# Reading wq in eight transfers of sixteen rows instead of one of 128

## The chip, the cores and the metric

The kernel runs on one core of a Trainium2 chip. The metric is the device time of one execution in microseconds. The profile is that of one execution, taken by the hardware profiler. Engines in it: PE is TensorE (PEld its weight loads), DVE VectorE, ACT ScalarE, POOL GpSimd, SP SyncE, which here only issues transfers. A "q" behind an engine's name is its sequencer. The core has sixteen DMA engines, which all queues share. SP's transfers are on one queue (q1 in the profile), ACT's on another (q10).

## The reference

A gated mix of two blocks for a single decode token, batch 2, all in bf16. Block A is attention over a cache of 16,384 positions with 32 heads of 128; block B is an MLP with a layer norm. The caches dominate the bytes: K and V have 268 MB each.

```python
def _A_ref(x, k_cache, v_cache, wq, wo):
    B, Sq, D = x.shape                       # 2, 1, 1024
    H, Dh = 32, 128
    q = transpose((x @ wq).reshape(B, Sq, H, Dh), 0, 2, 1, 3)
    scores = jnp.einsum("bhqd,bhkd->bhqk", q, k_cache) * (Dh ** -0.5)
    p = softmax(scores, axis=-1)
    o = jnp.einsum("bhqk,bhkd->bhqd", p, v_cache)
    return transpose(o, 0, 2, 1, 3).reshape(B, Sq, H * Dh) @ wo

g = sigmoid((x * gate_w).sum(-1, keepdims=True))
a = _A_ref(x, A_k_cache, A_v_cache, A_wq, A_wo)
b = _B_ref(x, B_w1, B_w2, B_w3, B_w4)        # layer norm, gelu, shifts, two more products
return g * a + (1 - g) * b
```

wq is 1024 x 4096 bf16, 8.39 MB; wo is as large. w2 has 2.10 MB, w3 and w4 7.34 MB each, w1 2.10 MB.

## The kernel before, in words

**Memory.** One tile, `mem`, holds 128 partitions of five cells of 32 KB. A unit of K or V (two heads of one batch) is 8.39 MB, that is 64 KB a partition, two cells. K of batch 0 uses cells 0 and 1, K of batch 1 cells 1 and 2, V cells 3 and 4. So K of the other batch can be loaded as soon as DVE has turned the half of K that lies in cell 1. wq lies first in cells 3 and 4 (64 KB a partition: partition p holds rows 8p to 8p+7 of wq), then w3, then V. w2 is in cell 2.

**Transfers.** SP issues wq (line 91, in `load_weight`), then K of head pair 0 and batch 0, called K(0,0) here (line 109), and waits with w3 (line 91) until PE has read wq out of the same cells. Then come K(0,1), V(0,0) and so on, each as soon as its cells are free. ACT's queue takes x and the gate's weights (lines 97 and 98) and w2. Transfers of one queue are worked off in the order in which they were issued.

**The start.** PE turns x, then waits for wq and multiplies (`rows4`, line 203, 64 matmuls for q). ACT and DVE bring q into the form that the scores need. Then a chain of small steps computes the gate, the layer norm, the product with w2, the second layer norm and xn2T; it ends on DVE with the copy `lane_b`, ahead of the first transpose of K. Each engine takes its instructions in program order (`in_order`).

**The loop.** For each of 16 head pairs and both batches: DVE transposes K by chunks (line 427), PE multiplies with q (line 433), a softmax on DVE, ACT and PE, then PE multiplies with V (line 487). The first unit runs ahead of the loop. The last pair also loads wo, w4 and w1 into freed cells, and PE computes the output from these (line 394).

**Waiting.** Tile's own tracking gives each transfer a semaphore. A tail load of the kernel uses another way, in `load_tail`: the transfer raises a semaphore of the kernel's own, is taken out of the tracking by a group, PE waits on the semaphore by hand, and `declare_fence` says which instruction of PE closes the group. The change uses the same for wq.

Of the kernel before, what the change touches and what calls it, by code (L numbers as in the profile page):

```python
# [23 lines left out]
def kernel(  # L24
# [15 lines left out]
    nc = tc.nc  # L40
    P = nc.NUM_PARTITIONS
    B, Sq, D = A_x.shape
    _, H, Sk, Dh = A_k_cache.shape
# [3 lines left out]
    KC = D // P  # L47
# [32 lines left out]
    def region(cell, elements, offset=0):  # L80
        at = cell * CELL + offset
        return mem[:, at : at + elements]

    def load_weight(W, cell, offset=0, pieces=None, queue=nc.sync):
        K, N = W.shape
        dst = region(cell, K // P * N, offset)
        src = W.rearrange("(p r) n -> p (r n)", p=P)
        r = 0
        for n in pieces or (K // P,):
            at = slice(r * N, (r + n) * N)  # L90
            queue.dma_start(out=dst[:, at], in_=src[:, at])
            r += n
        return dst.rearrange("p (r n) -> p r n", n=N)

    wq = load_weight(A_wq, 3)
    rows = const.tile([B + 1, D], BF16, name="rows")
    nc.scalar.dma_start(out=rows[0:B], in_=A_x.rearrange("b s n -> (b s) n"))
    nc.scalar.dma_start(out=rows[B : B + 1], in_=gate_w.unsqueeze(0))
# [14 lines left out]
    def load_v(hp, b, cell=V_CELL):  # L113
# [7 lines left out]
        out=ident_s[:], in0=ident_f[:], scalar1=-scale, scalar2=None, op0=ALU.mult  # L121
# [10 lines left out]
        out=mask4[:], in_=mask4[:], compare_op=ALU.is_ge, fill=0.0,  # L132
# [3 lines left out]
        out=mask4[:], in_=mask4[:], compare_op=ALU.is_ge, fill=0.0,  # L136
# [11 lines left out]
        out=lmat[:].rearrange("p (g h k) -> p g h k", h=2, k=4),  # L148
        in_=hm2[:].unsqueeze(1).unsqueeze(3).to_broadcast([P, P // 8, 2, 4]),
# [5 lines left out]
        out=lane[:],  # L155
        in_=ident_f[:].rearrange("p (c k) -> p k c", k=QP),
# [5 lines left out]
    for g in range(Q4):  # L162
        nc.vector.tensor_scalar(
            out=spread[:, g],
# [4 lines left out]
    oacc = [ops.tile([P, 4 * Dh], FP32, name=f"oacc{k}") for k in range(2)]  # L169
# [19 lines left out]

    def rows4(acc, actT, weight, R, at, n, G, added=None):
        for g in range(Q4 if added is not None else 0):
            nc.tensor.matmul(
                acc[QP * g : QP * g + B, 0:n],
                lhsT=ident_b[0:B, 0:B],
                rhs=added[:, g * G + at : g * G + at + n],
                start=True,
                stop=False,
            )  # L200
        for r in range(R):
            for g in range(Q4):
                nc.tensor.matmul(  # L203
                    acc[QP * g : QP * g + B, 0:n],
                    lhsT=actT[:, r, :],
                    rhs=weight[:, r, g * G + at : g * G + at + n],
                    start=(r == 0 and added is None),
                    stop=(r == R - 1),
                )

    def turned(wide, C):
        t = mlp.tile([P, C, QP], FP32, tag="turn", name="turn")
        nc.vector.transpose(  # L213
            out=t[:].rearrange("p c k -> p (c k)"), in_=wide.rearrange("p c k -> p (c k)")
        )
        return t[:, :, 0:B]

    def layer(actT, weight, k, added=None):
        rows4(oacc[k], actT, weight, KC, 0, G1, G1, added)
        wide = mlp.tile([P, KC, QP], FP32, tag="wide", name="wide")  # L220
        nc.scalar.activation(
            out=wide[:], in_=oacc[k][:, 0:G1].rearrange("p (i r) -> p r i", r=KC), func=ACTF.Copy
        )
        return turned(wide[:], KC)
# [11 lines left out]
    nc.vector.tensor_copy(out=rowsT[:], in_=rows_ps[:])  # L236
    xT = rowsT[:, :, 0:B]

    for k in range(2):
        rows4(oacc[k], xT, wq, KC, k * 4 * 512, 512, 512)  # L240
    NV = 4
    qb = const.tile([P, 2, 2, 2, B, NV], BF16, name="qb")
    for k in range(2):
        wide = mlp.tile([P, 16, QP], FP32, tag="wide", name="wide")
        nc.scalar.activation(  # L245
            out=wide[:].rearrange("p (c e) i -> p c e i", e=2),
            in_=oacc[k][:].rearrange("p (c i e) -> p c e i", i=QP, e=2),
# [15 lines left out]
    for e in range(2):  # L263
        half = slice(e * HALF, (e + 1) * HALF)
        nc.vector.tensor_copy(
            out=qdu[half].rearrange("p u v -> p (u v)"),
            in_=qdps[half, e].rearrange("p k g n -> p (k g n)"),
# [83 lines left out]
    for shift in (1, -1, 2, -2):  # L351
# [10 lines left out]
        out=x1_rows[:], in_=oacc[1][:, 0:G1], func=ACTF.Copy, scale=omg_row[:, 0:1]  # L362
# [3 lines left out]
    def mlp_third(w3):  # L366
        for k in range(2):
            rows4(oacc[k], xn2T, w3, KC, k * (G3 // 2), G3 // 2, G3)
        wide3 = mlp.tile([P, FC, QP], FP32, tag="wide", name="wide")
        for k in range(2):  # L370
            nc.scalar.activation(
                out=wide3[:, :, k * (QP // 2) : (k + 1) * (QP // 2)],
                in_=oacc[k][:, 0 : G3 // 2].rearrange("p (i r) -> p r i", r=FC),
                func=ACTF.Copy,
            )
        h2 = gelu_T(turned(wide3[:], FC), FC)
        nc.vector.tensor_tensor(out=h2T[:], in0=h2[:], in1=spread_batch(omg, FC), op=ALU.mult)
# [340 lines left out]
```

## Time and profile before

| what | us |
|---|---|
| median of three runs | 1329.3 (1329.28 to 1329.56) |
| profiled execution | 1329.34 |
| its span, first to last instruction | 1327.5 |
| wq, from issue to landing | 26.0 |
| w3, from issue to landing | 32.1 |
| K, from issue to landing, median of 32 | 27.8 |
| SP waiting on DVE's transposes before it issues K, 31 times | 509.1 |

The core read 572.53 MB from HBM in this execution, 431 GB/s over the span. A DMA share of 1.00 means that the sixteen DMA engines worked all the time in a stretch. Packets count in the window in which they start, so a window of one or two microseconds can show a share above 1 or a rate above the mean. An idle time is put down to what came last before the waiting instruction; idle time of an engine that is not the bottleneck costs nothing.

### The profile page before, as it was taken

The numbers are of one execution on the slowest core, as the hardware profiler recorded it, in microseconds if no ns is written. First come the engines' busy times: TensorE is split into PE (matmuls) and PEld (weight loads), VectorE is DVE, ScalarE is ACT, GpSimd is POOL, SyncE is SP. The second block draws the span as 40 slices with busy tenths as digits, with TensorE's granted clock in tenths as the row PEclk, the third lists the DMA queues.
The fourth block names the chain that finished last, engine by engine and source line by source line (L and its number), as shares of the span: only waits on it lengthen the run. The fifth ranks groups of instructions, "written<-read, shape, count | busy, mean of one in ns | idle before, by whom it ended". The sixth has DMA issues, their size and how long they took to land. (4 is left out here: it accounts for less than half of the span.)

```text
span 1327.5 us, 12951 instructions
## 1 busy us (share of the span) xinstructions
PE 753.8 (57%) x4948; PEld 329.0 (25%) x4948; DVE 648.1 (49%) x507; ACT 131.9 (10%) x205; POOL 11.9 (1%) x48
## 2 busy tenths in 40 slices
PE   2555566655556665555666555566655556665553
PEld 0222222222222222222222222222222222222222
DVE  1654445554444555444455544445554444555420
ACT  0011111011111100111110011111001111100110
POOL 0000000000000000000000000000000000000000
PEclk9677788777778877777887777788777778877777
DMA  9999999999999999999999999999999999999998
GB/s 411 441 435 421 433 440 425 436 436 440 423 434 438 430 434 432 440 423 436 436 438 427 432 440 425 434 438 438 425 434 438 429 432 436 440 423 436 436 430 373
DMA packets 10676, 572.68 MB, mean 431 GB/s; under 512 B 1189, under 2 KB 1189, under 8 KB 1578
## 3 DMA queue, kind: packets, MB, share of 16 engines
q1 hardware_dynamic: 10512, 570.43, 99.4%
q10 hardware_dynamic: 154, 2.11, 0.4%
q8 instruction: 8, 0.13, 0.0%
q14 instruction: 2, 0.02, 0.0%
HBM read 572.53 MB, written 0.00 MB: 431 GB/s over the span
## 5 line engine op out<-in xcount | busy, mean ns | idle before, releaser
L433 PE MATMUL S<-KT,qw 128*128 128x512 bf16 x2048 | 545.5, 416 | 357.1 <-DVE KT L427 357.0
L427 DVE STREAM_TRANSPOSE KT<-mem 128x2048 f32<-128x2048 f32 x256 | 570.6, 2282 | 261.7 <-DMA mem<-in_A_k_cache_dram 205.6
L433 PEld LDWEIGHTS <-qw 128*128 128x128 bf16 x2048 | 215.9, 105 | 678.6 <-issue 473.6
L487 PE MATMUL oacc<-mem,pt 128*8 128x512 bf16 x2048 | 117.9, 383 | 6.6 <-DMA mem<-in_A_v_cache_dram 6.6
L458 ACT ACTIVATE Dm<-ident_s,m 128x128 f32<-128x128 f32 x32 | 12.9, 402 | 970.1 <-PE oacc L487 943.5
L471 ACT ACTIVATE pt<-St,nb 64x256 bf16<-64x256 f32 x64 | 89.7, 1401 | 60.3 <-DVE nb L469 59.4
L509 DVE TENSOR_SCALAR o_all<-misc,g_rep 128x2 f32 (+1 forms) x32 | 7.0, 219 | 162.1 <-PE misc L505 162.1
L480 PE MATMUL misc<-rs,lmat 128*128 128x1 f32 x64 | 18.8, 363 | 107.9 <-ACT pt L471 61.3
L487 PEld LDWEIGHTS <-pt 128*8 128x8 bf16 x2048 | 47.3, 87 | 74.4 <-issue 22.4
L505 PE MATMUL misc<-lane,osb 128*128 128x2 f32 x256 | 33.5, 253 | 45.3 <-ACT osb L500 45.3
L481 DVE RECIPROCAL rinv<-misc 128x1 f32<-128x1 f32 x32 | 5.4, 168 | 108.6 <-PE misc L480 60.5
L454 DVE STREAM_TRANSPOSE St<-S 128x512 f32<-128x512 f32 x32 | 22.9, 717 | 66.4 <-PE L487 64.5
L505 PEld LDWEIGHTS misc<-lane,osb 128*128 128x128 f32 x256 | 31.2, 192 | 61.1 <-ACT osb L500 31.7
L480 PEld LDWEIGHTS misc<-rs,lmat 128*128 128x128 f32 x64 | 16.1, 312 | 114.3 <-ACT pt L471 64.8
L500 ACT ACTIVATE osb<-oacc,rinv 128x512 f32<-128x512 f32 x32 | 22.0, 687 | 87.2 <-PE oacc L487 87.2
L471 ACT ACTIVATION_READ_ACCUMULATOR pt<-St,nb 64x1 f32 x64 | 30.6, 478 | 0.0
L381 POOL TENSOR_TENSOR qw<-qdu,mask 128x16 bf16<-128x16 bf16 x32 | 7.3, 261 | 1135.8 <-PEq L677 1074.7
L469 DVE TENSOR_REDUCE nb<-misc 64x1 f32<-64x64 f32 x64 | 14.2, 222 | 6.1 <-PE misc L464 3.6
L213 DVE STREAM_TRANSPOSE turn<-wide 128x512 f32<-128x512 f32 (+2 forms) x4 | 3.0, 745 | 26.3 <-ACT wide L245 21.3
L464 PE MATMUL misc<-Dm,ones_f 128*128 128x128 f32 x64 | 15.7, 329 | 0.0
L203 PE MATMUL oacc<-mem,rowsT 128*2 128x512 bf16 x64 | 6.2, 570 | 15.7 <-DMA mem<-in_A_wq_dram 15.7
L456 DVE TENSOR_REDUCE m<-St 128x1 f32<-128x256 f32 x32 | 13.4, 420 | 1.1
(98 smaller groups left out, 85.1 us busy)
## 6 DMA issues: line engine op xcount, KB each, us to landing
mem<-in_B_w_dram SPq DMA_DIRECT2D x1, 7168.0 KB, 32.1
mem<-in_B_w_dram SPq DMA_DIRECT2D x1, 4096.0 KB, 41.2
mem<-in_B_w_dram SPq DMA_DIRECT2D x1, 2304.0 KB, 32.2
mem<-in_B_w_dram ACTq DMA_DIRECT2D x1, 2048.0 KB, 33.1
mem<-in_B_w_dram SPq DMA_DIRECT2D x1, 1280.0 KB, 35.0
mem<-in_B_w_dram SPq DMA_DIRECT2D x1, 768.0 KB, 33.5
mem<-in_A_k_cache_dram SPq DMA_DIRECT2D x32, 27.8
mem<-in_A_v_cache_dram SPq DMA_DIRECT2D x32, 32.4
```

The lines of the kernel that those rows point to most:

```text
L427: nc.vector.transpose(out=kt[:], in_=Kc.rearrange("p j d -> p (j d)").bitcast(FP32))
L433: nc.tensor.matmul(S, lhsT=qw[b][:, v, NG - 1 - m : NG - 1 - m + P], rhs=ktb[:, half * GT : (half + 1) * GT, w, :, e], start=(first and n ...
L454: nc.vector.transpose(out=st[:].rearrange("p j r -> p (j r)"), in_=S[:])
L456: nc.vector.tensor_reduce(out=m[:], in_=st[:, :, 0:NG], axis=AX.XY, op=ALU.max)
L458: nc.scalar.activation(out=Dm[:], in_=ident_s[:], func=ACTF.Copy, scale=m[:, 0:1])
L464: nc.tensor.matmul(R_ps[:], lhsT=ones_f[:], rhs=Dm[:], start=True, stop=True)
L469: nc.vector.tensor_reduce(out=nb[rows], in_=R_ps[rows, rows], axis=AX.X, op=ALU.min)
L471: nc.scalar.activation(out=pts[b][rows, :, e, :].rearrange("p (m a) k -> p a k m", a=GT // 4), in_=st[rows, :, 0:NG].rearrange("p (a k) m ...
L480: nc.tensor.matmul(tot_ps[:], lhsT=lmat[:], rhs=rs[:], start=True, stop=True)
L487: nc.tensor.matmul(oacc[b][QP * q : QP * q + 8, :], lhsT=pts[b][:, g].rearrange("p h k -> p (h k)"), rhs=V[:, 4 * g : 4 * g + 4, :].rearra ...
L500: nc.scalar.activation(out=osb[:], in_=oacc[b][:], func=ACTF.Copy, scale=rinvs[b][:, 0:1])
L505: nc.tensor.matmul(ot[:], lhsT=osb[:, k * Dh : (k + 1) * Dh], rhs=lane[:, k : k + 5 : 4], start=(k == 0), stop=(k == 3),)
```

## The change

wq is no longer read by `load_weight` in one transfer of 128 rows (one row of 65,536 bytes a partition), but by a loop of eight transfers on the same queue, SP's. Transfer k takes the sixteen partitions k, k+8, ..., k+120, and the same rows of the source. All eight count on one semaphore, `wq`, 16 each; PE waits for 128 before the first matmul with wq. The transfers and the matmuls are in the group `wq`, so Tile adds no waits between them, and the last matmul closes the group for the loads that come into these cells later. The bytes, their place and the matmuls are the same.

```diff
-    wq = load_weight(A_wq, 3)
+    wq_all = region(3, KC * H * Dh)
+    wq_src = A_wq.rearrange("(p r) n -> p (r n)", p=P)
+    wq_sem = tc.alloc_semaphore("wq")
+    ROWS_OF = P // 16
+    for k in range(ROWS_OF):
+        dma = nc.sync.dma_start(out=wq_all[k:P:ROWS_OF], in_=wq_src[k:P:ROWS_OF])
+        dma.then_inc(wq_sem, 16)
+        tc.no_tile_sem_insts.add(dma.ins.name)
+        tc.add_to_no_dep_group("wq", dma.ins)
+    wq = wq_all.rearrange("p (r n) -> p r n", n=H * Dh)
...
-    def rows4(acc, actT, weight, R, at, n, G, added=None):
+    def rows4(acc, actT, weight, R, at, n, G, added=None, group=None):
...
-                nc.tensor.matmul(
+                mm = nc.tensor.matmul(
...
+                if group is not None:
+                    tc.declare_no_dep(mm.ins, group=group, reason="own semaphore")
+        return mm
...
+    nc.tensor.wait_ge(wq_sem, 16 * ROWS_OF)
     for k in range(2):
-        rows4(oacc[k], xT, wq, KC, k * 4 * 512, 512, 512)
+        mm = rows4(oacc[k], xT, wq, KC, k * 4 * 512, 512, 512, group="wq")
+    tc.declare_fence(mm.ins, group="wq")
```

## The prediction

> **What bounds the kernel now.** I read the page's busy shares and its DMA lines first, then stretches of the span for the rate stage by stage, then the first 60 us in order of time, then SP's own waits. The page, its span and DMA lines:
>
> ```profile
> span 1327.5 us, 12951 instructions
> PE 753.8 (57%) x4948; PEld 329.0 (25%) x4948; DVE 648.1 (49%) x507; ACT 131.9 (10%) x205; POOL 11.9 (1%) x48
> ...
> DMA  9999999999999999999999999999999999999998
> ...
> q1 hardware_dynamic: 10512, 570.43, 99.4%
> q10 hardware_dynamic: 154, 2.11, 0.4%
> ```
>
> No compute engine passes 57%, while the sixteen DMA engines are taken for 99.8% of their span by SP's queue (q1) and ACT's (q10). The chain that ended last gives DMA only 32%, because it often steps through compute to an issue that did not hold the engines up; the shares of the DMA engines decide here. Stretches of the span (columns: stretch, us, busy time of each engine, PE clock, DMA share, GB/s):
>
> ```profile
> 1.80:26.80 25.00, 0.63 (x8) 0.65 (x9) 4.15 (x12) 1.28 (x1) 2.11 (x5) 1.00 1.02 431
> 26.80:48.00 21.20, 11.48 (x114) 5.84 (x114) 6.12 (x31) 2.22 (x5) 1.63 (x3) 0.71 0.99 426
> 48.00:65.00 17.00, 13.35 (x47) 5.15 (x47) 15.02 (x7) 0.00 (x0) 0.00 (x0) 0.77 1.01 439
> 65.00:300.00 235.00, 139.51 (x871) 59.66 (x872) 124.17 (x93) 24.02 (x38) 1.37 (x6) 0.80 1.00 433
> 300.00:800.00 500.00, 289.50 (x1799) 126.03 (x1792) 255.26 (x182) 50.66 (x78) 3.17 (x14) 0.78 1.00 434
> ```
>
> The rate is one flat ceiling, 433 to 434 GB/s at a DMA share of 1.00, whether wq, a cache or a weight is read. So a row of 65,536 B takes one engine 65,536 / (433/16 GB/s) = 2.42 us. wq has 128 such rows, 8 an engine: 19.4 us. w2 (2.10 MB) takes 4.8 us, K(0,0) 19.4 us and w3 (7.34 MB) 17.0 us. Nothing later can make up for time lost here: from 65 to 1284 us the engines have no idle share to take it back from.
>
> The first 60 us in order of time (start, duration, engine, line, operation; in brackets the idle time before and what ended it):
>
> ```profile
> 0.80 0.38 SPq L91 DMA_DIRECT2D mem<-in_A_wq_dram  x1
> ...
> 1.25 0.42 SPq L109 DMA_DIRECT2D mem<-in_A_k_cache_dram  x1
> ...
> 26.89 6.17 PE L203 MATMUL oacc<-mem,rowsT 128*2 128x512 bf16 x64 [15.69 <-DMA mem<-in_A_wq_dram]
> ...
> 32.89 0.33 SPq L91 DMA_DIRECT2D mem<-in_B_w_dram  x1
> ...
> 48.04 4.51 DVE L427 STREAM_TRANSPOSE KT<-mem 128x2048 f32<-128x2048 f32 x2 [0.58 <-DMA mem<-in_A_k_cache_dram]
> ...
> 59.14 0.33 SPq L109 DMA_DIRECT2D mem<-in_A_k_cache_dram  x1
> ```
>
> wq lands at 26.8 us, PE projects q for 6.2 us, and only then does SP issue w3 into the same cells (32.89). K(0,0) covers that gap: it lands at 48.0. K(0,1) is issued at 59.14, and w3 lasts until 65.0 (32.89 plus the 32.1 us to landing in the list of DMA issues), a margin of 5.9 us.
>
> **The change, part by part.** The sum is against the profiled execution: 1327.5 us of span and 1.8 around it make 1329.34, 0.04 above the median of 1329.3, so terms are added to 1329.3. About 0.2% (2.7 us) is what I count as different from no change.
>
> 1. *Issues on SP.* One issue of 0.38 us becomes eight: 8 x 0.38 = 3.1 us, or, by the five tail issues at 1286.81 that together hold SP for 3.42 us (0.68 each), 5.5 us. K(0,0), behind them on SP, goes from 1.25 to between 4 and 6 us; its first row is wanted at about 26 us. The eighth transfer leaves SP by 6 us at the latest and is wanted after seven rows, 17 us. ACT's three issues stay. Cost 0; the cover is what the engines already hold, and if it were gone the cost would be 2.7 to 5.1 us.
>
> 2. *Completion.* The transfers count on one semaphore, and PE waits for 128 in the place where it waited for wq's landing. Queued behind that wait on PE are the 64 matmuls of L203, then all of PE; ACT's copies at L245 and SP's w3 wait for those matmuls as before. Seven more completions an engine: at the seam from wq to K(0,0), near 26 us, the shares 1.02 and 0.99 leave at most 1% of 46 us, 0.5 us, for that seam and every other. I take 0.1 us for the seven together, ends 0 and 3.5 (each a whole 0.5).
>
> 3. *The start.* The windows of 1 us below count a row where it starts.
>
> ```profile
> 1.00:2.00 1.00, 0.00 (x0) 0.00 (x0) 0.50 (x6) 0.00 (x0) 0.79 (x6) 1.00 1.84 594
> 2.00:3.00 1.00, 0.00 (x0) 0.00 (x0) 0.96 (x3) 0.00 (x0) 1.00 (x3) 1.00 1.29 459
> 3.00:4.00 1.00, 0.00 (x0) 0.00 (x0) 0.99 (x2) 0.00 (x0) 0.91 (x2) 1.00 0.00 0
> 4.00:5.00 1.00, 0.00 (x0) 0.00 (x0) 0.87 (x4) 0.00 (x0) 0.00 (x0) 1.00 0.61 262
> 5.00:6.00 1.00, 0.00 (x0) 0.00 (x0) 0.86 (x2) 0.35 (x1) 0.00 (x0) 1.00 1.81 786
> ```
>
> Sixteen rows (1,053 KB) start between 1 and 3 us, about 2.0 in the mean, and the next sixteen between 4 and 6, about 5.1: 3.1 us for a round that later takes 2.42. Shorter transfers might let all engines start sooner. The most that can come back is the 0.7 us of that round and some 0.4 us of spread: -1.1. The other end is 0; I take -0.1, since nothing shows that the slow first round comes from the number of rows in a transfer.
>
> 4. *Which rows are on their way together.* This is the large term. Now each engine has eight rows of the 128. After the change the sixteen engines write partitions k, k+8, ... k+120 at once, first for k=0, then 1, up to 7. If the 27.1 GB/s belongs to the engine, it makes no difference which partitions these are: 0. If it belongs to a path into a group of partitions, and rows 8 apart meet two to a path, each pair halves: a round takes 4.84 us, eight take 38.7, +19.4. The rows do not hold such a meeting, so both ends come from the 2.42 us. I take the upper. The ceiling is the same for every tensor read, to 0.3%, which points away from the memory that is read and to something on the way into the chip; and sixteen streams that all run at exactly one sixteenth for 1,280 us look like sixteen separate paths that are now used evenly. The edit changes the set of partitions that take turns on those paths, and half as many in use is the simplest uneven case. w2's rows (4.8 us) run beside wq. Where they use the idle half, up to 4.8 us come back (+14.6); where they too are halved, 4.8 are added (+24.2).
>
> [...]
>
> 5. *What is late next.* wq's landing, K(0,0)'s and w3's all move by the same amount. From wq's landing to the end of the small chain before the first score (the DVE copy lane_b at 47.28) are 20.5 us, and K(0,0) lands 21.2 after wq. If w2 is through earlier, that chain can overtake K by about 1 us and put K(0,1)'s issue 1 us later, inside the margin of 5.9. Cost 0; beyond the margin it would count in full.
>
> Sum: 0 + 0.1 - 0.1 + 19.4 + 0 = +19.4, so 1348.7 us.
>
> **The rivals.**
> - *The engine alone sets the rate (other side).* Then terms 1 to 3 are all: from -1.1 to +0.6, 1328.2 to 1329.9, about 1329.2. For it: the trace never shows two rows competing. Against: the same flat ceiling whatever is read. It decides in the first round: it holds if the second set of rows starts near 5 us, and falls if near 8.
> - *Each transfer pays its start again.* From issue (0.80) to the mean first start (2.0) are 1.2 us, and 0.7 more are lost in the first round: 7 x 1.9 = 13.3, 1342.6. Against: K(0,0) followed wq on the same queue at full share, and eight issues leave faster (0.45 us apart) than rows are eaten (2.42). [...]
> [...]
>
> **How the numbers follow.** Shared paths 0.79, engine alone 0.15, start paid again 0.03, two rows an engine 0.03. Predicted: the first, 1348.7, with its own range 1343.9 to 1353.5 (+14.6 to +24.2). I give that range nine tenths of its case, 0.71, so the whole range has to reach down to the second case: 1328.2 to 1353.5. Faster by over 0.2% would need 2.7 us and term 3 holds 1.1 at most: 0.01, for something unseen. Within 0.2%: 0.14 + 0.03 = 0.17. Slower: 0.79 + 0.03 = 0.82.
>
> **What would show it.** Right: in the 1 us windows the rows of the second round start near 7 us; over wq's stretch the rate is near 220 GB/s with a DMA share still at 1.0, since halved rows occupy their engines for longer; PE's L203 starts near 46 us instead of 26.89, w3 leaves SP near 52, and from there on everything is as before, 19 us later. Wrong: L203 still near 27 us (engine alone), or a DMA share well below 1 between 2 and 46 us (starts paid again). I would also be wrong in size if w2's rows fill the idle half (L203 nearer 42), or if the shift found at L203 were not the same at the end, which would mean idle DMA time that I could not see.

## The result, and the profile after

The changed kernel takes 1351.59 us (median of six runs, 1351.12 to 1352.15), the kernel before 1329.42. The ratio is 1.0167, with a 95% interval of 1.0157 to 1.0177: 22.2 us slower.

The page of the changed kernel, its span, its DMA lines and the rate by slices of 1/40 of the span:

```profile
span 1349.3 us, 12958 instructions
...
DMA  9899999999999999999999999999999999999998
GB/s 249 311 436 436 432 432 435 433 435 433 435 435 435 435 435 433 433 424 433 433 435 435 429 433 435 433 435 433 435 435 435 435 435 433 433 422 435 433 435 375
```

Apart from the last slice (375, and 373 in the kernel before), only the first two differ from the rest. There the DMA engines are busy for at least nine and eight tenths of the time, nearly as anywhere else, and move 249 and 311 GB/s. The busy share alone would have shown little; share and rate have to be read together. The stretches of the span (the last two columns are DMA share and GB/s):

```profile
1.80:37.00 35.20, 0.62 (x8) 0.57 (x8) 4.15 (x12) 1.28 (x1) 2.11 (x5) 1.00 1.01 238
37.30:47.50 10.20, 0.00 (x0) 0.00 (x0) 0.00 (x0) 0.00 (x0) 0.00 (x0) 1.00 1.00 206
...
51.00:66.00 15.00, 8.93 (x98) 4.21 (x90) 4.30 (x20) 1.72 (x4) 0.71 (x1) 0.75 1.01 438
...
87.00:300.00 213.00, 121.61 (x788) 52.82 (x788) 105.13 (x84) 24.03 (x38) 1.37 (x6) 0.79 1.00 434
```

While wq runs beside w2, the engines move 238 GB/s at a share of 1.01. In the last 10 us of wq, when w2 is through, it is 206 GB/s at a share of 1.00: 12.9 GB/s an engine, so that a row of 65,536 B takes 5.09 us in place of 2.42. From 51 us on everything is as before. In order of time:

```profile
0.80 5.05 SPq L100 DMA_DIRECT2D mem<-in_A_wq_dram  x8
...
49.44 6.35 PE L212 MATMUL oacc<-mem,rowsT 128*2 128x512 bf16 x64 [40.29 <-DMA mem<-in_A_wq_dram]
...
55.84 0.33 SPq L91 DMA_DIRECT2D mem<-in_B_w_dram  x1
...
70.12 4.50 DVE L441 STREAM_TRANSPOSE KT<-mem 128x2048 f32<-128x2048 f32 x2
```

The matmuls with wq (L203 before, L212 now) start at 49.44 in place of 26.89, 22.6 us later. The first transpose of K starts at 70.12 in place of 48.04, 22.1 later, and the span ends 21.8 later. The loss arises in the first 50 us and is carried to the end, 0.8 us smaller than at the matmuls.

### The profile page after: what moved, and what is told of

It reads as the page before. It is cut to its first block, busy times and chain, and to the rows that moved or that the text cites. A ratio compares the mean times of both kernels' runs of the same rounds, so it can differ in the third digit from the quotient of the medians.

```text
span 1349.3 us, 12958 instructions
## 1 busy us (share of the span) xinstructions
PE 754.8 (56%) x4948; PEld 329.0 (24%) x4948; DVE 647.8 (48%) x507; ACT 132.0 (10%) x205; POOL 11.9 (1%) x48
## 5 line engine op out<-in xcount | busy, mean ns | idle before, releaser
L472 ACT ACTIVATE Dm<-ident_s,m 128x128 f32<-128x128 f32 x32 | 12.9, 402 | 967.2 <-PE oacc L501 942.1
L494 PE MATMUL misc<-rs,lmat 128*128 128x1 f32 x64 | 18.7, 362 | 107.9 <-ACT pt L485 61.3
L212 PE MATMUL oacc<-mem,rowsT 128*2 128x512 bf16 x64 | 6.4, 583 | 40.3 <-DMA mem<-in_A_wq_dram 40.3
```

The source lines that it names most:

```text
L472: nc.scalar.activation(out=Dm[:], in_=ident_s[:], func=ACTF.Copy, scale=m[:, 0:1])
L494: nc.tensor.matmul(tot_ps[:], lhsT=lmat[:], rhs=rs[:], start=True, stop=True)
```

## Experiments

The theory was that what costs is which partitions are written at the same time: sixteen paths into the core's memory, each shared by some partitions. The profile names neither such a path nor the engine of a row: the runs show the rates of sets of partitions, and what is said of paths below is how the theory reads these rates. Which partitions share a path is an assumption of each expectation. Three rivals: each of the eight transfers costs something (a start, a completion on the shared semaphore); the distance between the rows in the source costs; the loss belongs to the cold start. All kernels compute the whole output. "Before" on the same chip was 1329.3 to 1329.6 us each time. The first kernel below was run eleven times, each of the others once; the six runs of the change spread over 1.0 us, so differences below 1 us between single runs are not read here. "Rate over share" is the rate divided by the DMA share: what all sixteen engines would move if they were busy all the time.

### Eight transfers of all partitions

```diff
     for k in range(ROWS_OF):
-        dma = nc.sync.dma_start(out=wq_all[k:P:ROWS_OF], in_=wq_src[k:P:ROWS_OF])
+        part = slice(k * H * Dh, (k + 1) * H * Dh)
+        dma = nc.sync.dma_start(out=wq_all[:, part], in_=wq_src[:, part])
```

> wq in eight transfers on the same semaphore, but each of all 128 partitions and one eighth of the columns (8 KB a row). Shared paths: what costs is which partitions are written together, so nothing is lost: 1328.5 to 1330.0 us, L203 starts near 27 us, DMA rate 433 GB/s from 2 to 27 us. Transfers (each of the eight pays a start or a completion, 22 us / 7 = 3.1 us each): about 1351 us, L203 near 49 us.

Measured: 1329.56 us (eleven runs), ratio to before 1.0001, interval 0.9992 to 1.0010. The stretch with wq in this run:

```profile
2.00:26.00 24.00, 0.60 (x8) 0.65 (x8) 4.05 (x11) 1.28 (x1) 1.92 (x4) 1.00 1.01 420
```

Same number of transfers, same bytes in each, same semaphore and same wait, and no loss. Number of transfers and way of counting are out as causes. L213, the matmuls with wq here, start at 27.90, 1.0 us later than before; the first transpose of K starts at 48.59 in place of 48.04, so K(0,0) covers about half of that, and the time is within the interval of no change.

### Sixteen neighbours, and steps of 4

```diff
-        dma = nc.sync.dma_start(out=wq_all[k:P:ROWS_OF], in_=wq_src[k:P:ROWS_OF])
+        part = slice(16 * k, 16 * k + 16)
+        dma = nc.sync.dma_start(out=wq_all[part], in_=wq_src[part])
```

> Eight transfers of sixteen rows as in the change, but each of sixteen neighbouring partitions (16k to 16k+15). Shared paths with four neighbours to a path: four engines share one, a row takes 4 x 2.42 = 9.7 to 10.2 us, wq 77 to 82 us at 103 to 109 GB/s, so 1387 to 1397 us with what w2 adds. Transfers: 1351 us as the change. Reading (rows 512 KB apart in the source are what is slow): rows are 64 KB apart here, so less than the change, 1330 to 1351 us.

Measured: 1387.95 us, 58.6 more than before. The stretches of this run, wq beside w2 and then wq alone:

```profile
2.00:62.00 60.00, 0.63 (x8) 0.57 (x8) 4.04 (x11) 1.28 (x1) 1.91 (x4) 1.00 0.98 130
62.00:80.00 18.00, 0.00 (x0) 0.00 (x0) 0.00 (x0) 0.00 (x0) 0.00 (x0) 1.00 1.04 117
```

Rate over share is 117/1.04 = 112 GB/s for wq alone, about a quarter of 433, as four engines on one path would have it. The rows are nearest to each other in the source here (65,536 bytes), and the loss is the largest of all, so a loss that grows with their distance falls too.

The next kernel takes partitions 4 apart in one half of the partitions:

```diff
-        dma = nc.sync.dma_start(out=wq_all[k:P:ROWS_OF], in_=wq_src[k:P:ROWS_OF])
+        at = 64 * (k % 2)
+        dma = nc.sync.dma_start(
+            out=wq_all[at : at + 64][k // 2 : 64 : 4], in_=wq_src[at : at + 64][k // 2 : 64 : 4]
+        )
```

> Eight transfers of sixteen rows, partitions 4 apart within the lower or the upper 64 (0, 4, ... 60, then 64, 68, ... 124, then from 1, and so on). Shared paths, if p and p+32 are on one path and p and p+64 are not: eight paths with two rows each, as the change: 1350.5 to 1353 us, L203 near 49 us. If p and p+32 were on different paths: 1329 to 1331 us. Transfers: 1351 us. Reading: rows 256 KB apart in place of 512, about half the loss, 1340 us.

Measured: 1350.91 us, L215 (wq) from 49.43. The first 12 us of wq, beside w2:

```profile
2.00:14.00 12.00, 0.63 (x8) 0.58 (x8) 4.04 (x11) 1.28 (x1) 1.91 (x4) 1.00 0.99 224
```

224/0.99 = 226 GB/s, and in time as the change: 21.5 us more than before, where the change has 22.2. The theory accounts for it if the sixteen rows in steps of 4 within 64 lie two to a path. The rows are half as far apart in the source as in the change, and the loss is not halved.

### The same transfers 32 partitions further up

```diff
-    for k in range(ROWS_OF):
-        dma = nc.sync.dma_start(out=wq_all[k:P:ROWS_OF], in_=wq_src[k:P:ROWS_OF])
+    parts = [slice(32 + j, 96 + j, 4) for j in range(4)]
+    parts += [slice(at + j, at + 32, 2) for j in range(2) for at in (0, 96)]
+    for part in parts:
+        dma = nc.sync.dma_start(out=wq_all[part], in_=wq_src[part])
```

> Eight transfers of sixteen rows. The first four take partitions 32+j to 92+j in steps of 4, the last four 0 to 31 and 96 to 127 in steps of 2. Shared paths: 32 to 95 in steps of 4 meets all sixteen paths once, so the first four run at 2.42 us a row, and the last four, two rows to a path, at 4.8 to 5.1: half the loss, 1339.5 to 1342 us, L203 near 38 us, 433 GB/s up to about 13 us and 206 to 230 behind it. Transfers: 1351 us. Reading: the first four are 256 KB apart as in the run with steps of 4 in one half, and would be as slow as there.

Measured: 1340.17 us, 10.8 more than before, half the loss; L214 starts at 38.43. The stretches of this run:

```profile
2.00:14.00 12.00, 0.61 (x8) 0.66 (x8) 4.04 (x11) 1.28 (x1) 1.91 (x4) 1.00 1.10 459
...
24.00:35.00 11.00, 0.00 (x0) 0.00 (x0) 0.00 (x0) 0.00 (x0) 0.00 (x0) 1.00 0.90 191
```

The first four transfers, with w2 beside them, run at 459/1.10 = 417 GB/s, the last four at 191/0.90 = 212. Together with the run before, this is the sharpest pair. Sixteen rows in steps of 4, from partition 0 or from partition 32: the same size, count, step and distance in the source. From 0 they run at about half the rate (224/0.99 = 226 in the same 12 us), from 32 at the full one. What differs is the set of partitions, and with it the set of source rows that are read together: no run here moves the one without the other. Against a meeting in the memory that is read speaks the next run, where the rows of the source lie 57,344 bytes apart instead of 65,536 and the rate is halved all the same (206 GB/s).

### w3 instead of wq

wq in one transfer again, and w3 read in the manner of the change, at a time when the queue is full. (Tile takes the strided slices for overlapping with K's cells, so the first unit's transposes and K(0,1) are put into the group too.)

```diff
+        nc.tensor.wait_ge(w3_sem, 16 * 8)
...
-    w3 = load_weight(B_w3, 3)
...
+    for k in range(8):
+        dma = nc.sync.dma_start(out=w3_all[k:P:8], in_=w3_src[k:P:8])
+        dma.then_inc(w3_sem, 16)
...
```

> wq in one transfer as before; w3 instead in eight transfers of sixteen partitions 8 apart, on a semaphore of its own, at 46 us, with the queue full. Shared paths: eight rounds of 57,344 B at 206 to 218 GB/s, 4.2 to 4.45 us in place of 2.12: +17 to +19, 1346.3 to 1348.7 us, L203 for q still near 27 us. If the loss belongs to the cold start or to wq: 1329.0 to 1330.0 us.

Measured: 1349.33 us, 19.9 more than before on the same chip. The loss needs neither the cold start nor wq. It is 0.6 us above the top of what I had expected. The first transpose of K, and the stretch with w3:

```profile
49.85 4.50 DVE L434 STREAM_TRANSPOSE KT<-mem 128x2048 f32<-128x2048 f32 x2 [3.11 <-DMA mem<-in_A_k_cache_dram]
...
48.00:78.00 30.00, 16.51 (x64) 6.41 (x63) 18.92 (x10) 0.40 (x1) 0.00 (x0) 0.84 1.04 214
```

214/1.04 = 206 GB/s, the rate at the end of wq in the change: 7.34 MB in 35.6 us in place of 17.0, or +18.7. Some 1.2 us are not in that. K(0,0) lands at 49.85 in place of 48.04, 1.8 us later: part of the loss arises before this stretch, where K's last rows and, it seems, w3's first run together; from 36 to 50 us rate over share is 383/1.08 = 355 GB/s. That they met on the same paths there is argued, not shown.

### Eight rows on eight engines

```diff
-    for k in range(ROWS_OF):
-        dma = nc.sync.dma_start(out=wq_all[k:P:ROWS_OF], in_=wq_src[k:P:ROWS_OF])
+    for k in range(2 * ROWS_OF):
+        at = 32 * (k % 4) + k // 4
+        part = slice(at, 32 * (k % 4) + 32, 4)
+        dma = nc.sync.dma_start(out=wq_all[part], in_=wq_src[part])
...
-    nc.tensor.wait_ge(wq_sem, 16 * ROWS_OF)
+    nc.tensor.wait_ge(wq_sem, 32 * ROWS_OF)
```

> wq in sixteen transfers of eight rows, partitions 4 apart within 32 neighbours: eight paths, one row to each. Shared paths, and eight rows on eight engines, always the same eight: no two rows meet, so each row takes 2.42 us, but eight engines carry all of wq: 16 x 2.42 = 38.7 us in place of 19.4, 1347.5 to 1350.5 us, with a DMA share well below 1 between 27 us and the issue of w3 near 52, and rate over share at 433 GB/s throughout. If few partitions are slow by themselves, without two engines meeting: rate over share near 206 to 220 GB/s, as in the change, and more than 1351 us.

Measured: 1357.76 us, 7.3 us above the first range. The time alone would fit the other case (more than 1351 us). L214 starts at 56.02, and w3 leaves SP at 61.05, not near 52. The stretches decide between the cases, and tell what was missed:

```profile
24.00:32.00 8.00, 0.00 (x0) 0.00 (x0) 0.00 (x0) 0.00 (x0) 0.00 (x0) 1.00 1.16 262
44.00:57.00 13.00, 0.98 (x12) 0.41 (x16) 0.00 (x0) 0.00 (x0) 0.00 (x0) 1.00 0.47 202
```

From 44 to 57 us, half of the engines' time is used (share 0.47) and rate over share is 202/0.47 = 430 GB/s, 26.9 an engine: the full rate for an engine, with eight rows to a transfer. So few partitions are not slow by themselves, and the other case falls. What the halved runs have beside that is, by the theory, two engines on one path. From 24 to 32 us rate over share is only 262/1.16 = 226. All engines are busy there (share 1.16), more than twice the share from 44 to 57 us: the others, it seems, had gone on to K(0,0), which SP had issued behind wq at 11.68 us, and it would fit the theory that their rows met wq's on the same paths; I had taken them to be out of the way. That K was under way there, and that the meeting is between K and wq, is argued from the issue order and not tried by itself.

### w2 behind wq

```diff
-    w2 = load_weight(B_w2, 2, queue=nc.scalar)
+    w2 = load_weight(B_w2, 2)
```

> The change, with w2 issued on SP behind wq in place of ACT's queue beside it. Is the 2.8 us over the forecast w2 in the crowd? If w2's rows are slowed beside wq's (0.8 to 1.3 us in place of 0.61): each wq row alone takes 5.09 us (206 GB/s, as in the last 10 us of wq in the change), wq 40.7 us, L203 near 44 us, w2 then at 433 GB/s, in sum 1350.5 to 1352 us, about as the change. If w2's rows ran for nothing in the idle half: 4.8 us more than the change, 1355 to 1357 us.

Measured: 1350.80 us, L212 from 44.29, as expected. The stretches of this run, wq alone and what follows:

```profile
2.00:40.00 38.00, 0.62 (x8) 0.56 (x8) 3.34 (x11) 1.28 (x1) 2.13 (x4) 1.00 1.07 221
44.00:90.00 46.00, 26.14 (x177) 11.55 (x178) 23.92 (x39) 2.23 (x5) 1.63 (x3) 0.78 1.03 444
```

221/1.07 = 207 GB/s for wq by itself, 8.39 MB in 40.6 us in place of 19.4: +21.2 without any help from w2. So w2 neither fills an idle half for nothing, nor is it needed for the loss.

### Two other splits by partition

Two halves, and four transfers of 32 rows:

```diff
-    for k in range(ROWS_OF):
-        dma = nc.sync.dma_start(out=wq_all[k:P:ROWS_OF], in_=wq_src[k:P:ROWS_OF])
+    for k in range(2):
+        part = slice(64 * k, 64 * k + 64)
+        dma = nc.sync.dma_start(out=wq_all[part], in_=wq_src[part])
...
-    nc.tensor.wait_ge(wq_sem, 16 * ROWS_OF)
+    nc.tensor.wait_ge(wq_sem, 32)
```

> wq in two transfers of 64 rows, partitions 0 to 63, then 64 to 127. Shared paths, with p and p+32 on one path and the two halves on different ones: each transfer meets eight paths with two engines on each, as the change: 1350 to 1352 us, L203 near 49 us. Transfers or steps between partitions as the cause: two large transfers of neighbouring partitions cost nothing, 1329.0 to 1330.5 us.

Measured: 1353.84 us, 24.4 more than before, and 1.8 above the range given. Two large transfers of neighbours are a little worse than the eight of the change. In this run wq and w2 go at 222 GB/s with a share of 1.04 from 2 to 48 us, that is 213; in the change they go at 232 with a share of 1.01 from 2.2 to 47.5 us, that is 230. Why the halves do worse these runs do not show.

```diff
-    for k in range(ROWS_OF):
-        dma = nc.sync.dma_start(out=wq_all[k:P:ROWS_OF], in_=wq_src[k:P:ROWS_OF])
+    for k in range(4):
+        dma = nc.sync.dma_start(out=wq_all[k:P:4], in_=wq_src[k:P:4])
...
-    nc.tensor.wait_ge(wq_sem, 16 * ROWS_OF)
+    nc.tensor.wait_ge(wq_sem, 64)
```

> wq in four transfers of 32 rows, partitions k, k+4, ... k+124, which meet all sixteen paths with two rows each. If an engine takes two rows that follow each other (8e+k, then 8e+k+4), each round still has partitions 8 apart, two engines to a path: 1350 to 1352 us, L203 near 49 us. If rows go to the engine that owns the path, as they seem to for 128 rows: nothing is lost, 1329.0 to 1330.5 us.

Measured: 1329.79 us beside 1329.46 before. No loss. The stretch with wq in this run:

```profile
2.00:26.00 24.00, 0.63 (x8) 0.57 (x8) 3.34 (x11) 1.28 (x1) 2.13 (x4) 1.00 1.04 437
```

437/1.04 = 420 GB/s, as before (431/1.02 = 422). By the theory, then, an engine's two rows are not neighbours in the list: 8e+k and 8e+k+4 would put partitions 8 apart into each round, which the change shows at half the rate (206 GB/s). How the rows are dealt out to the engines is not shown; the profile does not name the engine of a row.

## Why the prediction came out as it did

The forecast was 1348.7 with 1328.2 to 1353.5 around it; measured 1351.6. The sign and the place are the predicted ones, the runs fit the predicted mechanism, and the size of the loss was 2.8 us short. That the rate would be halved, no row of the kernel before could show: the prediction took two engines to a path as the simplest uneven case, and that choice, not a reading of the trace, made the number come close. Its signs came somewhat late: the matmuls with wq start at 49.44 in place of 46, and w3 leaves SP at 55.84 in place of 52.

1. *Issues on SP.* Right: the eight issues hold SP for 5.05 us, inside the 3.1 to 5.5 given, and K(0,0) leaves at 5.89, long before it is wanted.
2. *Completion.* Right: the run with eight transfers of all partitions has the same seven more completions, and takes 0.2 us more than before, inside its interval of no change. The range for the engine alone counted only +0.6 for terms 1 to 3, although this term by itself was given an end of +3.5; nothing in the forecast hangs on it.
3. *The start.* Right that nothing comes of it. Windows of 1 us of the changed kernel:

```profile
1.00:2.00 1.00, 0.00 (x0) 0.00 (x0) 0.50 (x6) 0.00 (x0) 0.79 (x6) 1.00 0.02 4
2.00:3.00 1.00, 0.00 (x0) 0.00 (x0) 0.96 (x3) 0.00 (x0) 1.00 (x3) 1.00 4.78 1049
...
6.00:7.00 1.00, 0.00 (x0) 0.00 (x0) 0.17 (x2) 0.93 (x1) 0.00 (x0) 1.00 0.33 66
7.00:8.00 1.00, 0.00 (x0) 0.00 (x0) 0.00 (x0) 0.00 (x0) 0.00 (x0) 1.00 1.63 395
8.00:9.00 1.00, 0.48 (x8) 0.51 (x8) 0.00 (x0) 0.00 (x0) 0.00 (x0) 1.00 3.93 852
```

All sixteen rows start between 2 and 3 us, a little later than before, and the next sixteen after 6 us, most of them after 8 (w2's first rows are counted here as well). The point named to decide the main rival, a second round near 5 us or near 8, fell to 8.

4. *Which rows are on their way together.* This is the term that was mis-sized: +19.4 was put down, by halving the rate of a path exactly. The runs show less than half the rate: 206 GB/s, reckoned over eight paths, are 25.8 GB/s a path, where a single engine had 27.1 in the kernel before (433/16). By that, wq alone takes 40.7 us and the term is +21.3. With w2 beside it the account comes out close to that: 10.49 MB of wq and w2 took 45.3 us (2.2 to 47.5, 232 GB/s), against 24.2 at 433, or +21.1. The traced run took 1351.12 us, 0.5 below the median, and its span is 21.8 us longer than before, so 0.7 us remain. I can only say where they may lie: the later first rows, and 47.5 to 51 us, where K's first rows may still run beside wq's last and the rate over share is 506/1.28 = 395. The bounds by w2, +14.6 and +24.2, held, and neither was reached: w2 neither filled the idle half for nothing nor was slowed with wq to the full.

5. *What is late next.* Right that it costs nothing: the transpose at 70.12 no longer waits for K, so the chain of small steps is now what ends last ahead of it. The delay that was feared from that did not come: K(0,1) leaves SP at 80.40, 21.3 us later than before, less than the shift at L203. w3 lands at 86.8 (55.84 plus 31.0 to landing), a margin of 6.4 us, and 21.8 later than the 65.0 of before, which is the shift at the end. The shift at L203, 22.6 us, is larger by 0.8.

Of the rivals, the engine alone as the limit falls by the changed kernel's own 206 GB/s at a share of 1.00; a start paid by each transfer falls by the run with eight transfers of all partitions (1329.56 us); two rows on each of eight engines falls because all sixteen engines were at work while the rate was half (share 1.00 at 206 GB/s).

The theory fits every run, the one with eight rows only with the meeting with K that is argued there. Rate over share was 206 GB/s in the change, 226 (beside w2) in the steps of 4 within 64, 213 (beside w2) in the halves and 112 with sixteen neighbours; it was 417 with steps of 4 from 32, 420 in the 32-row transfers and 420/1.01 = 416 by columns. That these sets differ in how many engines meet on a path is the theory's reading; only the rates were measured.

## What to carry to other kernels

In these runs wq came at the full rate in splits by columns (416 GB/s), into 32 rows 4 apart (420) and, for its first half, into sixteen rows 4 apart from partition 32 on (417). Splits into sixteen rows 8 apart (206), into halves (213) and into neighbours (112) did not have it, and on this kernel, whose DMA engines have a share of 1.00 (from 65 to 300 us before, from 87 to 300 after), the loss went straight to the end: 22.2, 24.4 and 58.6 us. Read rate over share, not the share: a halved rate with fully busy engines (206 GB/s at 1.00) came here with the set of partitions that were written together, a low share at a good rate (202 at 0.47) was missing work. If a split by partitions is wanted, measure the rate of its sets, and start from one that kept it, as the 32 rows 4 apart did.

## What the runs showed that I had not expected

- Reckoned over eight paths, two engines carry 25.8 GB/s together in the change, less than the 27.1 of one; reckoned over four, the four engines of the run with neighbours carry 112/4 = 28.1, more than one. If that reckoning holds, a path can do more than an engine drew here, and pairs lose some 5% to something that these runs do not show. Pairs only two partitions apart, the last four transfers of the run from 32 up, carried 212/8 = 26.5.
- 32 rows 4 apart lose nothing (1329.79 us), although 16 rows 8 apart lose 22.2: by the theory the engines take the 32 rows in an order that does not pair, which no trace shows.
- Two halves of 64 partitions, the split that looks most harmless, were the dearest of the three splits of wq that ran at about half the rate throughout: +24.4 us in a single run, beside 22.2 and 21.5.
- Engines that had no part in a transfer seem to have gone on to the next one in the queue (share 1.16 from 24 to 32 us) and then to have got in the way of the first (226 GB/s): the eight-row run took 1357.76 us where 1347.5 to 1350.5 had been expected.
